# One 96-row transfer for each input chunk of a two-stage Fourier kernel, without zeroed gaps between its rows

## The chip, the cores and the metric

One core of a Trainium2 chip runs the kernel. The metric is the device time of one execution in microseconds; of several executions the median counts. Lower is better.

## The reference, cut to what is computed

A Fourier layer over 3008 positions (2 sequences, width 256) is followed by two feed-forward layers (6016 tokens, 256 to 2048 to 256):

```python
X = np.fft.rfft(x, axis=1)
Yr = Xr @ w_r - Xi @ w_i + b_r
Yi = Xr @ w_i + Xi @ w_r + b_i
# soft threshold of Yr and Yi at 0.01
y = np.fft.irfft(Y, n=x.shape[1], axis=1)
h = y @ w_in;   y = (h * np.cos(h)) @ w_out
h = y @ w_in2;  out = (h * np.clip(h + 3, 0, 6) / 6) @ w_out2
```

## The kernel before

The Fourier transform of length 3008 = 47 x 64 is done in two steps. The change touches the loads of the first one. For each sequence `b`, the input stands in memory as 96 rows (two groups `s` of 48, the even and the odd of each pair of columns) by 32 pairs by 256. It is read in 8 chunks of 4 pairs, numbered `a` = 0 to 15 over both sequences. A chunk has two pieces, `a_part(a, kc)`: four TensorE products (recorded as eight) of the chunk's rows with a trigonometric table `ta` of the same rows (line 544), one ScalarE eviction from PSUM (line 553) and, for the first sequence, one VectorE subtraction (line 555).

The table is block-diagonal: the row group `s` only meets the columns of its own `s`, and everything else in the table tile is zero. In the kernel before, the two row groups of a chunk are also put apart in the tile, rows 16 to 63 and 80 to 127 (kind 0) or rows 0 to 47 and 64 to 111 (kind 1), the kinds taking turns by pairs of chunks (`KINDS`, line 52). So each chunk takes two transfers of 48 rows (`load_x`, line 517), and the gap rows of both x and table are zeroed by VectorE, ScalarE and GpSimd before use (lines 568 to 596). The table of a pair of chunks also comes in two transfers, one per group (`load_ta`, line 526).

The first eight chunks (sequence 0) all have their own place: `x_big`, `x_ring[2]` and `ta_big`. They are loaded ahead and consumed one behind the other, pieces 0 to 15, before any other product. The next eight use rings of three (`XB`), are loaded by `load_next` and consumed one per step in `k2_step` (line 730), between the products `w_mm` (line 652), `b_mm` (674, 679) and `v_mm` (718).

The order of TensorE, SP and ScalarE is the program's own (`manual_schedule`, line 488); VectorE and GpSimd are left to the planner in this part. All loads but the first table pair, which ScalarE issues, are issued by SP in this order: x 0, x 1, table 2, x 2, x 3, table 4, x 4, x 5, table 6, x 6 (lines 597 to 603), two weights, x 7, two weights, then table and x of chunks 8 and 9, the constants, chunk 10, and the raw feed-forward weights. Before the first chunk, TensorE runs `WARM` products of the zeroed tile `warm` (line 607); no other work depends on them. After the Fourier part, the feed-forward layers run from about 160 us to the end as a sequence of products on TensorE (line 865).

Of the kernel before, what the change touches and what calls it, by code (L numbers as in the profile page):

```python
# [9 lines left out]
F32 = mybir.dt.float32  # L10
# [4 lines left out]
AF = mybir.ActivationFunctionType  # L15
# [6 lines left out]
NB, D, DFF = 2, 256, 2048  # L22
# [3 lines left out]
NPAIR = N2 // 2  # L26
TP = 2 * N1
ROWS = 2 * DOF
LAM = 0.01
TWO_PI = 2.0 * math.pi  # L30
YPAIRS = 4
A_CHUNKS = [4] * 8
NFC = DFF // 128
TILE = 128
WARM = 9
YT = YPAIRS * TP
NG = NB * NPAIR // YPAIRS

# [10 lines left out]
LASTC = 20  # L49
RATE_W = ((2, 1, 2), (1, 0, 1), (1, 1, 1), (0, 0, 0))  # L50
XB = 3
KINDS = (((16, 64), (80, 128), 128, ((0, 16), (64, 80)), (((0, 16), (64, 128)), ((0, 64), (64, 80)))), ((0, 48), (64, 112), 112, ((32, 64),), (((32, 64), (64, 128)), ((0, 64),))))
STAGED = [0] * 9 + [1, 2, 4, 5, 7, 8, 10] + [12] * 10
Y_EARLY = range(15, 18)
BIAS_DVE = range(13, 22)
# [25 lines left out]
def _tables():  # L81
    n1 = np.arange(N1)
    k2 = np.arange(NK2)
    ta = np.zeros((2, 48, NPAIR, NK2, 2))
    tg = np.zeros((2, NK2, 2, NPAIR, 2, N1))
    for i in range(NPAIR):
        for s in range(2):
            n = 64 * n1 + 2 * i + s
            c, sn = _trig(np.outer(n, k2), NSEQ)
            ta[s, :N1, i, :, 0] = c  # L90
            ta[s, :N1, i, :, 1] = -sn
            w = np.where(k2 == 0, 1.0, 2.0)[:, None] / NSEQ
            tg[s, :, 0, i, s, :] = w * c.T
            tg[s, :, 1, i, s, :] = -w * sn.T
    j = np.arange(N2)
    c, s = _trig(np.outer(j, j), N2)
    sg = np.where(j < N2 // 2, 1.0, -1.0)[None, :]
    f1 = np.zeros((2, N2, 2, N2))
    f1[0, :, 0], f1[1, :, 0] = c, s
    f1[0, :, 1], f1[1, :, 1] = -s, c  # L100
    f2 = np.zeros((2, N2, 2, N2))
    f2[0, :, 0], f2[1, :, 0] = sg * s, -sg * c
    f2[0, :, 1], f2[1, :, 1] = sg * c, sg * s
    g = np.zeros((2, N2, 2, 2, NPAIR))
    cc = c.reshape(N2, NPAIR, 2).transpose(0, 2, 1)
    ss = s.reshape(N2, NPAIR, 2).transpose(0, 2, 1)
    for z in range(2):
        g[0, :, z, 0], g[1, :, z, 0] = cc[:, z], -ss[:, z]
        g[0, :, z, 1], g[1, :, z, 1] = ss[:, z], cc[:, z]
    parts = []  # L110
    for m in (-f1, -f2, -g):
        parts += _split(m.reshape(128, 128))

    place = np.zeros((128, 128), dtype=np.float32)
    for row in (0, 32):
        place[row, :N2], place[row + 1, N2:] = -1.0, -sg[0]
    fg = np.concatenate(parts + [place], axis=1)
    return (
        ta.reshape(ROWS, NPAIR * 48).astype(np.float32),
        tg.reshape(ROWS, NPAIR * TP).astype(np.float32),  # L120
        np.ascontiguousarray(fg, dtype=np.float32),
    )
# [3 lines left out]
def fourier_moe_moe_kernel(ctx, tc, x, w_r, w_i, b_r, b_i, ta, tg, fg, win1, wout1, win2, wout2, out):  # L126
    nc = tc.nc
    pe, act, dve, sp = nc.tensor, nc.scalar, nc.vector, nc.sync

    def f32(ap):  # L130
        return ap.bitcast(F32)

    persist = ctx.enter_context(tc.tile_pool(name="persist", bufs=1))
# [352 lines left out]
    with ExitStack() as actx:  # L486
        apool = actx.enter_context(tc.tile_pool(name="apool", bufs=1))
        with tc.manual_schedule(engines={mybir.EngineType.PE, mybir.EngineType.SP, mybir.EngineType.Activation}):
# [2 lines left out]
            zl = apool.tile([128, NP, 2, 4, N2], F32R, name="zl")  # L491

            z1 = None
            x_big = persist.tile([128, 7, 4, D], F32, tag="zt", name="x_big")
            ta_big = persist.tile([128, 4, 2, 8, 48], F32, tag="wi0", name="ta_big")
            x_ring = [apool.tile([128, 4, D], F32, tag=f"x{r}", name=f"x_ring{r}") for r in range(XB)]
            ta_ring = [apool.tile([128, 2, 4, 48], F32, tag=f"ta{r}", name=f"ta_ring{r}") for r in range(XB)]
            a_list = []
            for b in range(NB):
                p0 = 0  # L500
                for n in A_CHUNKS:
                    a_list.append((b, p0, n))
                    p0 += n
            NA = len(A_CHUNKS)

            def place(a):

                if a >= NA:
                    r = (a - NA) % XB
                    return KINDS[r % 2], x_ring[r], ta_ring[r]  # L510
                xt = x_ring[XB - 1] if a == 0 else x_big[:, a - 1]
                return KINDS[a // 2 % 2], xt, ta_big[:, a // 2, :, 4 * (a % 2) : 4 * (a % 2) + 4]

            def load_x(a):
                b, p0, n = a_list[a]
                for s, (r0, r1) in enumerate(place(a)[0][:2]):
                    sp.dma_start(place(a)[1][r0:r1], x[b, 48 * s : 48 * s + 48, p0 : p0 + n, :])

            def load_ta(a, n, queue):
                p0 = a_list[a][1]  # L520
                kind, _, tt = place(a)
                if n > 4:
                    tt = ta_big[:, a // 2]
                for s, (r0, r1) in enumerate(kind[:2]):
                    src = ta[48 * s : 48 * s + 48, p0 * 48 : (p0 + n) * 48]
                    queue.dma_start(tt[r0:r1, s].rearrange("p i f -> p (i f)"), src)

            def load_next(a):
                if a < len(a_list):
                    load_ta(a, 4, sp)  # L530
                    load_x(a)

# [3 lines left out]
            def pool_zero(at):  # L536
                nc.gpsimd.memset(at, 0.0)

            def a_part(a, kc):
                b, p0, n = a_list[a]  # L540
                zp = h_bank(f"zp{a}_{kc}")
                (_, _, rows, _, _), xt, tt = place(a)
                for i in range(n):
                    pe.matmul(  # L544
                        zp[:, i * ROWS : (i + 1) * ROWS].rearrange("p (s f) -> p s f", s=2),
                        lhsT=xt[0:rows, i, kc * 128 : (kc + 1) * 128],
                        rhs=tt[0:rows, :, i],
                        start=True,
                        stop=True,
                    )  # L550
                src = zp[:, : n * ROWS].rearrange("p (n q f) -> p q f n", q=NP, f=4)
                dst = [z[:, :, kc, :, 2 * p0 : 2 * (p0 + n)] for z in ((zh, zl), (z1,))[b]]
                act.activation(dst[0], src, AF.Copy)
                if b == 0:
                    dve.tensor_tensor(dst[1], src, f32(dst[0]), op=ALU.subtract)

            def stage(q):

                act.activation(zh[:, q], z1[:, q], AF.Copy)
                pool_sub(zl[:, q], z1[:, q], f32(zh[:, q]))  # L560

            load_ta(0, 8, act)
            warm = persist.tile([128, 2, D], BF16, tag="r", bufs=5, name="warm")
            dve.memset(warm, 0.0)
            first = persist.tile([128, TILE], F32, tag="r", bufs=5, name="first")
            act.activation(first[:, 0:2], warm[:, 0, 0:2], AF.Sin)

            def x_zero(zero, kind, tiles):
                for r0, r1 in KINDS[kind][3]:
                    for t in tiles:  # L570
                        zero(t[r0:r1].rearrange("p n i e -> p (n i e)") if len(t.shape) == 4 else t[r0:r1].rearrange("p i e -> p (i e)"))

            def ta_zero(zero, kind, tile):
                for s in range(2):
                    for r0, r1 in KINDS[kind][4][s]:
                        zero(tile[r0:r1, s].rearrange("p i f -> p (i f)"))

            for t in (x_ring[2], x_big[:, 0]):
                for k, (r0, r1) in enumerate(KINDS[0][3]):
                    at = t[r0:r1].rearrange("p i e -> p (i e)")  # L580
                    if k == 0:
                        dve.memset(at, 0.0)
                    else:
                        act.activation(at, warm[r0:r1, 0, 0:1].to_broadcast([r1 - r0, 4 * D]), AF.Copy)
                if t is x_ring[2]:
                    ta_zero(dve_zero, 0, ta_big[:, 0])
            x_zero(pool_zero, 1, [x_big[:, 1:3]])
            ta_zero(pool_zero, 1, ta_big[:, 1])
            x_zero(pool_zero, 1, [x_big[:, 5:7]])
            ta_zero(pool_zero, 1, ta_big[:, 3])  # L590
            x_zero(pool_zero, 0, [x_big[:, 3:5]])
            ta_zero(pool_zero, 0, ta_big[:, 2])
            for r in range(XB):
                if r < XB - 1:
                    x_zero(pool_zero, r % 2, [x_ring[r]])
                ta_zero(pool_zero, r % 2, ta_ring[r])
            load_x(0)
            load_x(1)
            for a in range(2, NA):
# [5 lines left out]
            wp = psum.tile([128, 2, D], F32, tag="acc0", bufs=2, name="wp")  # L605
            for i in range(WARM):
                pe.matmul(wp, lhsT=warm[:, 0, 0:128], rhs=warm, start=True, stop=True)
# [212 lines left out]
    with tc.manual_schedule(engines=engines):  # L820
# [164 lines left out]
        for k in range(2 * G):  # L985
            n = HALF[k // STEPS % NJ]
            a, b, c, d = (bank(z, f"h{r}_{k}") for z, r in zip((0, 1, 2, 3) if k % 2 == 0 else (0, 3, 2, 1), "abcd"))
# [125 lines left out]
```

## Time and profile before

| | us |
|---|---|
| runs (three) | 1173.6, 1174.24, 1180.14 |
| median | 1174.24 |
| the profiled execution | 1174.77 |
| its span, first to last instruction | 1173.0 |

The profile shows one execution, with times from the start of the span. An engine's busy time counts neither issues of transfers nor waits. A stretch in which TensorE has gaps can be shortened; one without cannot, unless its own work shrinks. Transfers are shown by their issue on a queue (SPq, ACTq), by the median time from issue to landing, and by the rate at which all queues move bytes in a stretch. Names stand as out<-in.

### The profile page before, as it was taken

To read this page: it belongs to the slowest core of one execution; us is meant where nothing else is said; L and a number is where in the kernel's file an instruction comes from. 1 tells how busy PE (TensorE), PEld (TensorE's weight loads), DVE (VectorE), ACT (ScalarE), POOL (GpSimd) and SP (SyncE) were. 2 spreads that over 40 slices of the span, in tenths; PEclk is the share of its full clock that TensorE was granted. 3 is DMA by queue.
4 is the path that set the end of the run, shared out by engine and by line. 5 is a ranking of instruction groups with operands and counts; after the bars stand their busy time and mean duration, and the time that the engine had idled before them with its cause. 6 is when DMAs were issued, how large, how long until landed. Compare 5 with 4: busy or idle time off the path is not lost.

```text
span 1173.0 us, 15927 instructions
## 1 busy us (share of the span) xinstructions
PE 1154.8 (98%) x5363; PEld 965.8 (82%) x5363; DVE 766.5 (65%) x1096; ACT 814.7 (69%) x1548; POOL 814.3 (69%) x661
## 2 busy tenths in 40 slices
PE   8999989999999999999999999999999999999998
PEld 6887867778888888888888987888888888888897
DVE  5888877776679888988897677643343444433442
ACT  4677677777788888888788875565566556556554
POOL 5556636896787797888887786557757667577544
PEclk9999999999999999999999999999999999999999
DMA  9746639635413013104115420020020010100100
GB/s 202 194 115 178 190 95 292 211 100 171 136 55 110 34 59 130 37 18 149 37 39 187 172 93 1 1 72 1 1 72 1 19 54 1 68 1 1 37 1 32
DMA packets 48122, 98.71 MB, mean 84 GB/s; under 512 B 6436, under 2 KB 22952, under 8 KB 47400
## 3 DMA queue, kind: packets, MB, share of 16 engines
q1 hardware_dynamic: 47912, 97.54, 26.6%
q8 instruction: 42, 0.69, 0.3%
q14 instruction: 40, 0.33, 0.1%
q10 hardware_dynamic: 128, 0.15, 0.1%
HBM read 59.53 MB, written 38.14 MB: 83 GB/s over the span
## 4 chain that ended last, share of the span: by engine, by line
PE 85%; issue 4%; DMA 3%; POOL 3%; DVE 3%; ACT 2%; POOLq 0%; SPq 0%; ACTq 0%; DVEq 0%
PE acc L865 39%; PE hb L865 15%; PE ha L865 10%; PE hc L865 5%; PE hd L865 5%; PE pp L652 4%; POOL gl L175 3%; PE bp L679 2%; PE yp L391 2%; DMA x_big<-in_x_dram 1%; PE zp L544 1%; PE vp L718 1%; DVE r L841 0%; DMA ta_big<-in_ta_dram 0%; ACT tok L446 0%
## 5 line engine op out<-in xcount | busy, mean ns | idle before, releaser
L175 POOL TENSOR_TENSOR gl<-r,gh 128x512 fp32r<-128x512 f32 (+1 forms) x384 | 501.9, 1323 | 280.2 <-ACT gh L856 263.8
L865 PE MATMUL acc<-gh,wo 128*128 128x512 f32 (+1 forms) x1536 | 530.3, 386 | 0.0
L865 PEld LDWEIGHTS acc<-gh,wo 128*128 128x128 f32 x1536 | 288.6, 188 | 54.1
L865 PE MATMUL acc<-gl,wo 128*128 128x512 f32 (+1 forms) x768 | 296.1, 386 | 0.6 <-POOL gl L175 0.6
L865 PE MATMUL hb<-tok,wi 128*128 128x512 f32 (+1 forms) x864 | 241.7, 388 | 0.6 <-DVE hc L877 0.6
L856 ACT ACTIVATE gh<-r 128x512 fp32r<-128x512 f32 (+1 forms) x384 | 227.5, 615 | 0.4 <-PE acc L865 0.4
L865 PEld LDWEIGHTS hb<-tok,wi 128*128 128x128 f32 x864 | 161.3, 188 | 31.4 <-DVE hc L877 2.0
L877 DVE TENSOR_TENSOR hd<-p,hb 128x512 f32<-128x512 f32 (+1 forms) x96 | 65.8, 685 | 164.2 <-PE hb L865 159.3
L865 PEld LDWEIGHTS acc<-gl,wo 128*128 128x128 f32 x768 | 144.3, 188 | 27.6 <-POOL gl L175 1.0
L865 PE MATMUL ha<-tok,wi 128*128 128x512 f32 (+1 forms) x576 | 161.1, 388 | 2.2 <-ACT yo L410 2.2
L849 ACT ACTIVATE r<-r 128x512 f32<-128x512 f32 (+1 forms) x192 | 118.9, 619 | 57.3 <-DVE r L841 57.3
L865 PEld LDWEIGHTS ha<-tok,wi 128*128 128x128 f32 x576 | 108.0, 188 | 24.5 <-ACT yo L410 4.5
L449 POOL TENSOR_TENSOR tok<-st,tok 128x512 fp32r<-128x512 f32 (+1 forms) x77 | 97.7, 1282 | 2.9 <-ACT tok L446 2.9
L1006 ACT ACTIVATE p<-hc 128x512 f32<-128x512 f32 (+1 forms) x96 | 56.5, 588 | 58.4 <-PE hc L865 58.3
L843 ACT ACTIVATE r<-hd 128x512 f32<-128x512 f32 (+1 forms) x48 | 28.4, 591 | 78.1 <-PE hd L865 78.1
L997 ACT ACTIVATE hb<-ha 128x512 f32<-128x512 f32 (+1 forms) x96 | 55.2, 575 | 38.0 <-PE ha L865 37.8
L865 PE MATMUL hc<-tok,wi 128*128 128x512 f32 (+1 forms) x288 | 80.4, 387 | 1.2 <-DVE r L850 1.1
L865 PE MATMUL hd<-tok,wi 128*128 128x512 f32 (+1 forms) x288 | 79.7, 385 | 0.0
L877 DVE TENSOR_TENSOR hc<-p,hb 128x512 f32<-128x512 f32 (+1 forms) x96 | 65.4, 681 | 16.7 <-PE hb L865 15.9
L865 PEld LDWEIGHTS hc<-tok,wi 128*128 128x128 f32 x288 | 53.8, 188 | 12.5 <-DVE r L850 2.6
L865 PEld LDWEIGHTS hd<-tok,wi 128*128 128x128 f32 x288 | 54.1, 188 | 10.2
L850 DVE TENSOR_TENSOR r<-r,hb 128x512 f32<-128x512 f32 (+1 forms) x48 | 32.4, 675 | 40.9 <-ACT r L849 40.4
(144 smaller groups left out, 1712.8 us busy)
## 6 DMA issues: line engine op xcount, KB each, us to landing
st<-x_dram SPq DMA_DIRECT2D x18, 512.0 KB, 4.8
wi<-wi_dram SPq DMA_DIRECT2D x5, 1792.0 KB, 7.7
rawi<-in_win_dram SPq DMA_DIRECT2D x16, 512.0 KB, 4.0
rawo<-in_wout_dram SPq DMA_DIRECT2D x16, 512.0 KB, 3.8
u_dram<-v SPq DMA_DIRECT2D x48, 128.0 KB, 2.4
u_sb<-u_dram SPq DMA_DIRECT2D x16, 384.0 KB, 3.9
wo<-wo_dram SPq DMA_DIRECT2D x10, 512.0 KB, 8.0
x_dram<-o SPq DMA_DIRECT2D x20, 256.0 KB, 2.3
```

The source lines that it names most:

```text
L175: nc.gpsimd.tensor_tensor(out, x, y, op=ALU.subtract)
L391: pe.matmul(yp[:, i * TP : (i + 1) * TP], lhsT=u_sb[g][:, i, ec * 128 : (ec + 1) * 128], rhs=tg_sb[g][:, i * TP : (i + 1) * TP], start=Tru ...
L449: subtract(at(lo, t), src, f32(at(hi, t)), op=ALU.subtract)
L652: pe.matmul(pp.rearrange("p a e -> p (a e)"), lhsT=za[:, p, kc, 2 * (k2 % 2) : 2 * (k2 % 2) + 2, :].rearrange("p r n -> p (r n)"), rhs=wb[ ...
L843: act.activation(r, h, AF.Relu, bias=3.0, scale=1.0)
L849: act.activation(r, r, AF.Sin, bias=math.pi / 2, scale=1.0)
L850: dve.tensor_tensor(r, r, self.h[:, : self.n], op=ALU.mult)
L856: act.activation(gh[:, :n], self.r[:, :n], AF.Copy)
L865: pe.matmul(h[:, :n], lhsT=w, rhs=x, start=start and j == 0, stop=stop and j == 2, skip_group_check=True)
L877: dve.tensor_tensor(h[:, :n], r[:, :n], x[:, :n], op=ALU.add)
L997: act.activation(b[:, :n], a[:, :n], AF.Copy)
L1006: act.activation(p5[:, :n], c[:, :n], AF.Copy)
```

## The change

x and table rows of the two groups now stand directly behind each other, rows 0 to 47 and 48 to 95, in all chunks. A chunk of x is one transfer of 96 rows, and the x tiles have 96 rows and no gap rows. The table tiles keep zeros in the blocks off the diagonal: three memsets a tile, of which the first (rows 32 to 63 of group 0) overlaps rows that the load writes afterwards. The memsets of x are gone. `warm` is zeroed by GpSimd instead of VectorE, there are ten warm products instead of nine, and the table is laid out in memory pair by pair of chunks.

```diff
-WARM = 9
+WARM = 10
-        ta.reshape(ROWS, NPAIR * 48).astype(np.float32),
+        ta.reshape(ROWS, 4, NPAIR * 12).transpose(1, 0, 2).astype(np.float32),
...
-            x_big = persist.tile([128, 7, 4, D], F32, tag="zt", name="x_big")
+            x_big = persist.tile([ROWS, 7, 4, D], F32, tag="zt", name="x_big")
...
             def load_x(a):
-                b, p0, n = a_list[a]
-                for s, (r0, r1) in enumerate(place(a)[0][:2]):
-                    sp.dma_start(place(a)[1][r0:r1], x[b, 48 * s : 48 * s + 48, p0 : p0 + n, :])
+                sp.dma_start(place(a)[0], x[a // NA, :, 4 * (a % NA) : 4 * (a % NA) + 4])
 
             def load_ta(a, n, queue):
...
+                tt = place(a)[1] if n == 4 else ta_big[:, a // 2]
+                for s in range(2):
+                    src = ta[a % NA // 2, 48 * s : 48 * s + 48].rearrange("p (i f) -> p i f", f=48)
+                    queue.dma_start(tt[48 * s : 48 * s + 48, s], src if n == 8 else src[:, 4 * (a % 2) : 4 * (a % 2) + 4])
...
-                        lhsT=xt[0:rows, i, kc * 128 : (kc + 1) * 128],
-                        rhs=tt[0:rows, :, i],
+                        lhsT=xt[:, i, kc * 128 : (kc + 1) * 128],
+                        rhs=tt[:, :, i],
...
+            def ta_zero(zero, tile):
+                for r0, r1, s in ((32, 64, 0), (64, 96, 0), (0, 48, 1)):
+                    zero(tile[r0:r1, s].rearrange("p i f -> p (i f)"))
+
+            ta_zero(dve_zero, ta_big[:, 0])
             load_ta(0, 8, act)
             warm = persist.tile([128, 2, D], BF16, tag="r", bufs=5, name="warm")
-            dve.memset(warm, 0.0)
+            pool_zero(warm)
...
-            for t in (x_ring[2], x_big[:, 0]):
...
-            x_zero(pool_zero, 1, [x_big[:, 1:3]])
-            ta_zero(pool_zero, 1, ta_big[:, 1])
...
+            for k in (1, 2, 3):
+                ta_zero(pool_zero, ta_big[:, k])
             for r in range(XB):
-                if r < XB - 1:
-                    x_zero(pool_zero, r % 2, [x_ring[r]])
-                ta_zero(pool_zero, r % 2, ta_ring[r])
+                ta_zero(pool_zero, ta_ring[r])
```

## Rows read from the trace of the kernel before

**Rows 1.** The page's busy times: busy us (share of the span) xinstructions

```profile
PE 1154.8 (98%) x5363; PEld 965.8 (82%) x5363; DVE 766.5 (65%) x1096; ACT 814.7 (69%) x1548; POOL 814.3 (69%) x661
```

**Rows 2.** Windows: length, busy us by engine (xcount), PEclk, DMA share, GB/s

```profile
6.20:23.44 17.24, 15.21 (x128) 14.64 (x128) 8.59 (x16) 8.12 (x17) 11.45 (x22) 1.00 1.07 223
24.00:116.00 92.00, 91.03 (x462) 76.63 (x461) 76.46 (x110) 65.24 (x126) 50.83 (x40) 1.00 0.59 164
```

**Rows 3.** Chain of waits, 0 to 60 us: start us, us, what

```profile
4.95 5.09 DMA x_big<-in_x_dram
...
10.06 6.23 DMA x_big<-in_x_dram
...
16.30 5.26 DMA x_big<-in_x_dram
...
21.69 2.00 PE zp L544 x16
```

**Rows 4.** SP's own waits, 0 to 40 us: total us, times, longest us

```profile
SPq L526 <- DMA x_big<-in_x_dram: 3.6, 7, 0.7
```

**Rows 5.** Timeline, TensorE: start us, us, what xcount [idle before <-releaser]

```profile
1.20 4.02 PE L607 MATMUL wp<-warm 128*128 128x512 bf16 x9 [1.20 <-DVE warm L564]
6.21 2.00 PE L544 MATMUL zp<-ta_big,x_ring 128*128 128x96 f32 x16 [0.99 <-DMA ta_big<-in_ta_dram]
...
10.42 3.78 PE L544 MATMUL zp<-ta_big,x_big 112*128 112x96 f32 x32 [0.43 <-DVE zl L555]
...
21.69 2.00 PE L544 MATMUL zp<-ta_big,x_big 112*128 112x96 f32 x16 [0.80 <-DMA x_big<-in_x_dram]
23.47 0.48 PE L652 MATMUL pp<-wh,zh 128*128 128x512 f32 x1
```

**Rows 6.** Timeline of ScalarE, first unbroken run of evictions

```profile
8.24 0.49 ACT L553 ACTIVATE zh<-zp 128x384 fp32r<-128x384 f32 x1 [0.40 <-PE zp L544]
...
10.03 0.49 ACT L553 ACTIVATE zh<-zp 128x384 fp32r<-128x384 f32 x1 [0.40 <-PE zp L544]
```

**Rows 7.** DMA packets in 8 to 10 us, then in 1.8 to 23.4 us

```profile
DMA packets 132, 0.41 MB, mean 203 GB/s; under 512 B 33, under 2 KB 33, under 8 KB 132
...
DMA packets 2394, 4.76 MB, mean 220 GB/s; under 512 B 510, under 2 KB 1531, under 8 KB 2393
```

**Rows 8.** DMA in 32 to 33 us

```profile
DMA packets 101, 0.36 MB, mean 365 GB/s; under 512 B 12, under 2 KB 12, under 8 KB 101
```

**Rows 9.** A 96-row load; issues with KB and median us to landing; DMA 113.9:114.5

```profile
112.02 0.33 SPq L380 DMA_DIRECT2D u_sb<-u_dram  x1
...
u_sb<-u_dram SPq DMA_DIRECT2D x16, 384.0 KB, 3.9
...
x_big<-in_x_dram SPq DMA_DIRECT2D x14, 192.0 KB, 5.3
...
DMA packets 69, 0.21 MB, mean 356 GB/s; under 512 B 8, under 2 KB 22, under 8 KB 69
```

**Rows 10.** The start: timelines by engine, and one group with mean ns

```profile
0.74 0.90 ACTq L526 DMA_DIRECT2D ta_big<-in_ta_dram  x2
...
0.87 0.27 DVE L564 MEMSET warm<- 128x256 uint32 x1 [0.87 <-PEq L1099]
...
L534 DVE MEMSET ta_big<- 16x384 f32 x2 | 0.8, 378 | 0.1
...
0.74 1.80 POOL L537 MEMSET x_big<- 32x2048 f32 x1 [0.29 <-POOLq L1099]
2.48 1.36 POOL L537 MEMSET ta_big<- 32x384 f32 x3
```

**Rows 11.** DMA issues in 40 to 44 us: KB each, median us to landing

```profile
ta_ring<-in_ta_dram SPq DMA_DIRECT2D x1, 36.0 KB, 3.4
```

**Rows 12.** Busy times by stretch, later stages

```profile
176.60:180.00 3.40, 3.40 (x10) 2.64 (x9) 2.18 (x3) 2.94 (x7) 3.24 (x4) 0.50 0.96 330
...
140.00:260.00 120.00, 113.34 (x533) 91.16 (x532) 92.88 (x129) 89.25 (x171) 82.88 (x65) 0.99 0.58 185
```

More of the change, by code (lines that the diff above doesn't have):

```diff
@@ L31 @@
 YPAIRS = 4
-A_CHUNKS = [4] * 8
 NFC = DFF // 128
 TILE = 128
-WARM = 9
+WARM = 10
 YT = YPAIRS * TP
@@ L51 @@
 XB = 3
-KINDS = (((16, 64), (80, 128), 128, ((0, 16), (64, 80)), (((0, 16), (64, 128)), ((0, 64), (64, 80)))), ((0, 48), (64, 112), 112, ((32, 64),), (((32, 64), (64, 128)), ((0, 64),))))
 STAGED = [0] * 9 + [1, 2, 4, 5, 7, 8, 10] + [12] * 10
@@ L493, in fourier_moe_moe_kernel @@
             z1 = None
-            x_big = persist.tile([128, 7, 4, D], F32, tag="zt", name="x_big")
[L495 to L504, printed above, removed]
+            x_big = persist.tile([ROWS, 7, 4, D], F32, tag="zt", name="x_big")
+            ta_big = persist.tile([ROWS, 4, 2, 8, 48], F32, tag="wi0", name="ta_big")
+            x_ring = [apool.tile([ROWS, 4, D], F32, tag=f"x{r}", name=f"x_ring{r}") for r in range(XB)]
+            ta_ring = [apool.tile([ROWS, 2, 4, 48], F32, tag=f"ta{r}", name=f"ta_ring{r}") for r in range(XB)]
+            NA = NPAIR // 4
             def place(a):
@@ L509, in place @@
                     r = (a - NA) % XB
-                    return KINDS[r % 2], x_ring[r], ta_ring[r]
+                    return x_ring[r], ta_ring[r]
                 xt = x_ring[XB - 1] if a == 0 else x_big[:, a - 1]
-                return KINDS[a // 2 % 2], xt, ta_big[:, a // 2, :, 4 * (a % 2) : 4 * (a % 2) + 4]
+                return xt, ta_big[:, a // 2, :, 4 * (a % 2) : 4 * (a % 2) + 4]
             def load_x(a):
-                b, p0, n = a_list[a]
-                for s, (r0, r1) in enumerate(place(a)[0][:2]):
-                    sp.dma_start(place(a)[1][r0:r1], x[b, 48 * s : 48 * s + 48, p0 : p0 + n, :])
+                sp.dma_start(place(a)[0], x[a // NA, :, 4 * (a % NA) : 4 * (a % NA) + 4])
             def load_ta(a, n, queue):
[L520 to L526, printed above, removed]
+                tt = place(a)[1] if n == 4 else ta_big[:, a // 2]
+                for s in range(2):
+                    src = ta[a % NA // 2, 48 * s : 48 * s + 48].rearrange("p (i f) -> p i f", f=48)
+                    queue.dma_start(tt[48 * s : 48 * s + 48, s], src if n == 8 else src[:, 4 * (a % 2) : 4 * (a % 2) + 4])
             def load_next(a):
-                if a < len(a_list):
+                if a < 2 * NA:
                     load_ta(a, 4, sp)
@@ L539, in a_part @@
             def a_part(a, kc):
-                b, p0, n = a_list[a]
+                b, p0, n = a // NA, 4 * (a % NA), 4
                 zp = h_bank(f"zp{a}_{kc}")
-                (_, _, rows, _, _), xt, tt = place(a)
+                xt, tt = place(a)
                 for i in range(n):
@@ L560, in stage @@
                 pool_sub(zl[:, q], z1[:, q], f32(zh[:, q]))
+            def ta_zero(zero, tile):
+                for r0, r1, s in ((32, 64, 0), (64, 96, 0), (0, 48, 1)):
+                    zero(tile[r0:r1, s].rearrange("p i f -> p (i f)"))
+            ta_zero(dve_zero, ta_big[:, 0])
             load_ta(0, 8, act)
             warm = persist.tile([128, 2, D], BF16, tag="r", bufs=5, name="warm")
-            dve.memset(warm, 0.0)
+            pool_zero(warm)
             first = persist.tile([128, TILE], F32, tag="r", bufs=5, name="first")
             act.activation(first[:, 0:2], warm[:, 0, 0:2], AF.Sin)
[L568 to L576, printed above, removed]
-            for t in (x_ring[2], x_big[:, 0]):
[L579 to L586, printed above, removed]
-            x_zero(pool_zero, 1, [x_big[:, 1:3]])
-            ta_zero(pool_zero, 1, ta_big[:, 1])
[L589 to L592, printed above, removed]
+            for k in (1, 2, 3):
+                ta_zero(pool_zero, ta_big[:, k])
             for r in range(XB):
-                if r < XB - 1:
-                    x_zero(pool_zero, r % 2, [x_ring[r]])
-                ta_zero(pool_zero, r % 2, ta_ring[r])
+                ta_zero(pool_zero, ta_ring[r])
             load_x(0)
```

## Prediction

> **What bounds the kernel now.** I read the page's busy times first: TensorE is busy 1154.8 us of a span of 1173.0 [rows 1]. So a change outside TensorE can only give back TensorE's idle time. The busy times by stretch say where that is: from 24 us to 116 us it is busy 91.03 of 92.00, but from 6.20 to 23.44, the stretch that the diff edits, it is busy 15.21 of 17.24 while the DMA share is 1.07 [rows 2]. The chain of waits says what stands in the way there: three x transfers one behind the other, then TensorE from 21.69 [rows 3]. The reader is to see that each x transfer in that chain is issued within 0.02 us of the landing of the one before: a landing releases SP's next issue, so the stage is a closed loop at the pace of the DMA engines. SP's own waits say the same: seven waits of table issues for x landings, 3.6 us, lead the list [rows 4]. TensorE's order of time shows the stops: the first product at 6.21, then four stops, of which the first, before 10.42, and the last, before 21.69, stand there [rows 5]. Where nothing stops it, ScalarE's evictions start at 8.24 and, two pieces later, at 10.03: 0.895 us for each of the 16 pieces `a_part` [rows 6].
>
> **The price of an x chunk.** While only x pieces of 192 KB (48 rows) are in flight, the queues move 203 GB/s [rows 7]: 0.97 us for a half, 1.94 us for a chunk. TensorE needs two pieces for a chunk, 1.79 us, so the DMA is slower than TensorE, before the tables are counted. The same engines do better elsewhere: 365 GB/s at 32 us [rows 8]. The row closest to the new transfer is `u_sb`: 96 rows in one transfer, 384 KB, the same shape and row length. It lands 3.9 us after its issue, when a half of 192 KB takes 5.3 us in the loaded stage, and in the middle of the transfer issued at 112.02 the rate is 356 GB/s [rows 9]. (That rate may hold a little of the transfers around it: 22 of its 69 packets are small.) So a chunk costs between 1.08 us (at 365) and 1.94 us (no better than the halves). I take 1.10, the `u_sb` row, since shape and length are the same; but `u_sb` was nearly alone and x comes eight deep, so the upper bound stays in the range.
>
> [...]
>
> **Part by part.**
> *Loads.* x goes from two issues to one per chunk, about 0.45 us each by ScalarE's two [rows 10]; bytes do not change. Before the last chunk can be used, 8 chunks (3.15 MB), four table pairs (0.59 MB) and the first weights (0.26 MB) must pass: 4.0 MB. Fixed time around them, from the lone `u_sb`: 3.9 - 1.10 = 2.8 us [rows 9]. Before, at 220 GB/s over the stage [rows 7]: 0.75 + 2.8 + 18.2 = 21.75, and TensorE did restart at 21.69 [rows 5], so the model holds. After, at 356: 0.75 + 2.8 + 11.2 = 14.8. If TensorE starts at 6.0, it wants the chunk at 6.0 + 14 x 0.895 = 18.5. The loads then lie beside TensorE; that cover is gone below 4.0 MB / 14.95 us = 267 GB/s. What is late next is nothing before 18.5: TensorE's own pace becomes the bound.
>
> *First table.* Its zero rows 32 to 63 now overlap loaded rows 0 to 47, so ScalarE's first table issue waits for one VectorE memset (0.38 us, engine free at 0.87) [rows 10]: issue at 1.3 instead of 0.74, the second at 1.75 instead of about 1.2. Behind this wait in ScalarE's queue stand the activation table load and one tiny Sin; no eviction is due before 7. TensorE started 5.0 us after the old second issue; a lone table transfer takes 3.4 us [rows 11], so about 1.6 us was queueing at 220 GB/s; at 356 that is 1.0. Start: 1.75 + 3.4 + 1.0 = 6.15, with bounds 5.15 (alone) and 6.75 (as loaded as before). The ten warm products set a floor: GpSimd's memset of `warm` starts at 0.74 and costs between VectorE's 0.27 and the 0.45 of a 384-column one on GpSimd, and ten products at 4.02/9 = 0.447 us end near 5.6 [rows 5, 10]. I take 6.0. The tenth product, 0.45 us, fills time in which TensorE idled 0.99.
>
> *Later tables on SP.* Each first half waits for one GpSimd memset. GpSimd's big x memsets, the first from 0.74 for 1.80 us, are gone, so three memsets of 0.45 us a pair follow `warm` and the pairs 1 to 3 are zeroed at about 2.4, 3.8 and 5.1 [rows 10]. SP needs the first half-table of pair 1 at about 1.65, after two x issues, and the memset that it waits for (the first of three) ends near 1.6: at most 0.4 us for SP if the memsets run late, and behind that wait stand chunks 2 and 3, which TensorE wants at 9.6 and 11.4 and whose data lands 3 us earlier. The price is nothing; without that cover it would be the 0.4.
>
> *Memsets.* GpSimd sheds its x memsets, VectorE and ScalarE two each, all off TensorE's chain of [rows 3]: nothing, and nothing is uncovered. *Products* with 96 instead of 112 or 128 rows: 16 of 128 rows took 2.00 us at 6.21 and 16 of 112 rows 2.00 at 21.69 [rows 5], so the row count does not show: nothing, and by the same rows no loss either. *Table layout* by pairs: 1536-byte runs as before; taken as nothing, bounded by the table's whole 0.59 MB, 1.7 us, which the 3.7 us of slack above (18.5 - 14.8) covers.
>
> **The sum.** End of the stage: 6.0 + 16 x 0.895 + 0.1 = 20.4, against 21.69 + 2.00 = 23.69 [rows 5]; ScalarE must now squeeze two weight copies between evictions, +0.1. So -3.2 us. From 24 to 116 TensorE idles 1.0 us in all [rows 2], so the shift goes through; raw weights and constants are issued earlier too. Profiled execution: 1174.77 - 3.2 = 1171.6. It lies 0.5 over the median 1174.24, so **1171.0**.
>
> **The rivals.**
> *No relief (0.16).* Whole transfers also run at about 205 to 220 GB/s once several are queued, because the limit sits in the source rows or the queues. For it: x pieces never beat that in the stage. Against: `u_sb`. The last chunk is then again at about 21.7: time 1174.2, give or take 0.6.
> *Slower (0.05).* Transfers of 96 rows, queued one behind the other, crowd each other more than halves do, and a chunk costs more than two halves. It decides from 1.94 us per chunk; every 0.1 above costs 8 x 0.1 = 0.8 us at the same stops. At 2.4 us: 1174.2 + 3.7 = 1177.9. Against: `u_sb` [rows 9]. [...]
> *Table late (0.05).* The memset holds both halves of the first table and the queue is as full as before: the three memsets end near 2.2, 5.0 later is 7.2, the stage ends at 21.7, time 1172.2. The stage has no other place to lose it.
> *Later stages rearranged (0.08).* [...] Times from 1167.5 to 1176.
>
> **How the numbers follow.** The forecast has 0.66: 1170.5 to 1171.9 by the two starts, 5.6 and 6.75. With the late table, no relief and half of the last rival the range 1167.5 to 1174.8 holds a little over 8 in 10; the wrong-side rival lies outside. One per cent, about what a measurement of this kernel can tell from no change, is 11.7 us, more than every case gives: faster 0.02, same 0.96, slower 0.02.
>
> **What would show it.** Right: x landings under 5 us and over 267 GB/s between 3 and 15 us; zp without gaps from about 6.0, ending near 20.4; the first pp product near 20.2 instead of 23.47; all later stages 3 us earlier. Wrong: gaps before the fifth, ninth or thirteenth piece at 205 to 220 GB/s (no relief), a first product after 7 (table), or a shift of 3 us at 23 that is gone at 300 (later stages).

## The result

The changed kernel takes 1186.42 us (median of five runs, 1186.02 to 1188.27) against 1174.24 before; the ratio is 1.010, with a 95% interval of 1.0072 to 1.0128. The forecast was 3.2 us less, and the range up to 1174.8. The profiled execution took 1186.5 us, 11.7 more than that of before.

TensorE's timeline of the changed kernel, in the order of [rows 5] (start us, us, what xcount, idle before and who ended it):

```profile
1.32 4.45 PE L574 MATMUL wp<-warm 128*128 128x512 bf16 x10 [1.32 <-POOL warm L524]
7.60 2.13 PE L531 MATMUL zp<-ta_big,x_ring 96*128 96x96 f32 x16 [1.83 <-DMA ta_big<-in_ta_dram]
9.52 24.10 PE L531 MATMUL zp<-ta_big,x_big 96*128 96x96 f32 x112
33.33 0.77 PE L619 MATMUL pp<-wh,zh 128*128 128x512 f32 x1
```

The ten warm products end at 5.77, TensorE then stands idle for 1.83 us, and the last of the 16 pieces ends at 33.62, where it ended at 23.69 before. There are no more stops between chunks: at this pace of TensorE the loads keep up. What is longer is the work itself: 112 products in 24.10 us, which is 1.72 us a piece where [rows 6] gave 0.895. ScalarE's evictions, which follow the pieces, show the same, 1.71 us apart:

```profile
9.77 0.49 ACT L540 ACTIVATE zh<-zp 128x384 fp32r<-128x384 f32 x1 [0.53 <-PE zp L531]
11.47 0.49 ACT L540 ACTIVATE zh<-zp 128x384 fp32r<-128x384 f32 x1 [1.22 <-PE zp L531]
13.18 0.49 ACT L540 ACTIVATE zh<-zp 128x384 fp32r<-128x384 f32 x1 [1.22 <-PE zp L531]
```

The windows (length, busy us by engine, PEclk, DMA share, GB/s) say why:

```profile
6.00:9.30 3.30, 1.70 (x15) 1.73 (x16) 0.03 (x1) 0.49 (x1) 1.86 (x8) 1.00 1.04 260
9.40:36.60 27.20, 27.20 (x123) 26.62 (x123) 10.09 (x18) 8.73 (x18) 0.00 (x0) 0.50 0.71 193
36.70:128.70 92.00, 90.17 (x465) 76.56 (x464) 76.79 (x110) 64.59 (x125) 52.39 (x42) 1.00 0.50 144
```

TensorE's granted clock is 1.00, the upper level of this trace, in the row from 6.00 to 9.30, then 0.50, the lower level, for 27 us, with TensorE busy all the time, and 1.00 again from 36.65, 3.3 us after the wide weight products began. Before, nothing of the kind stands in this stage: the clock was 1.00 through [rows 2].

The views read 1.00 before 6 us too, but the warm products took as long as products of their shape do at 0.50. The weight products, 128x512 as well, took 628 ns each (median) under 0.50, from 33.85 to 36.05, and 389 to 397 ns under 1.00, from 37.4 to 60 us. The warm products (busy us, mean ns): the ten of the changed kernel, then five that ran between 5.0 and 5.9 us in a kernel with 13 of them (further down):

```profile
L574 PE MATMUL wp<-warm 128*128 128x512 bf16 x10 | 4.4, 631 | 1.3 <-POOL warm L524 1.3
```

```profile
L575 PE MATMUL wp<-warm 128*128 128x512 bf16 x5 | 1.2, 379 | 0.0
```

So the 1.00 that the views give at the start of this trace does not agree with the length of the products, 631 ns.

In the whole program the stage accounts for nearly all of it: its end moved by 9.9 us, the end of the first six weight products by 10.7 (36.24 against 25.59), the execution by 11.7.

The first table, for which that first product waits, took 5.7 us from issue to landing instead of 4.8 and was issued about 0.5 us later. DMA issues by ScalarE in the first 9 us, KB each, median us to landing, first of the changed kernel, then of the kernel before:

```profile
ta_big<-in_ta_dram ACTq DMA_DIRECT2D x2, 72.0 KB, 5.7
```

```profile
ta_big<-in_ta_dram ACTq DMA_DIRECT2D x2, 72.0 KB, 4.8
```

And the pace of the loads did rise, though not to the 356 GB/s of [rows 9]. DMA packets from 2 to 18 us, of the changed kernel, of the kernel before, and of the changed kernel's stretch with x transfers almost alone (10.2 to 12.2 us):

```profile
DMA packets 1892, 4.14 MB, mean 259 GB/s; under 512 B 303, under 2 KB 1139, under 8 KB 1892
```

```profile
DMA packets 1524, 3.42 MB, mean 214 GB/s; under 512 B 357, under 2 KB 863, under 8 KB 1524
```

```profile
DMA packets 138, 0.48 MB, mean 242 GB/s; under 512 B 18, under 2 KB 21, under 8 KB 138
```

### The profile page after: what moved, and what is told of

Its sections match the earlier page's. It is cut to its first block, busy times and chain, and to the rows that moved or that the text cites. A ratio compares the mean times of both kernels' runs of the same rounds, so it can differ in the third digit from the quotient of the medians.

```text
span 1184.7 us, 15891 instructions
## 1 busy us (share of the span) xinstructions
PE 1166.3 (98%) x5364; PEld 978.4 (83%) x5364; DVE 764.3 (65%) x1092; ACT 811.7 (69%) x1546; POOL 804.0 (68%) x652
## 4 chain that ended last, share of the span: by engine, by line
PE 85%; issue 4%; POOL 4%; ACT 2%; DVE 2%; DMA 2%; POOLq 0%; SPq 0%; ACTq 0%; DVEq 0%
PE acc L832 38%; PE hb L832 14%; PE ha L832 10%; PE hc L832 5%; PE hd L832 5%; PE pp L619 4%; PE zp L531 3%; POOL gl L173 3%; PE bp L646 2%; PE yp L389 2%; PE vp L685 1%; DMA ta_big<-in_ta_dram 0%; DVE r L808 0%; DMA wo<-wo_dram 0%; DMA tg_sb<-in_tg_dram 0%
## 5 line engine op out<-in xcount | busy, mean ns | idle before, releaser
L964 ACT ACTIVATE hb<-ha 128x512 f32<-128x512 f32 (+1 forms) x96 | 55.2, 575 | 37.5 <-PE ha L832 37.4
L832 PEld LDWEIGHTS hc<-tok,wi 128*128 128x128 f32 x288 | 53.7, 188 | 12.5 <-DVE r L817 2.5
L176 POOL TENSOR_TENSOR w<-cvai,cvbi 128x512 f32<-128x512 f32 x16 | 21.4, 1335 | 59.9 <-DVE cvbi L215 59.9
```

The source lines that it names most:

```text
L832: pe.matmul(h[:, :n], lhsT=w, rhs=x, start=start and j == 0, stop=stop and j == 2, skip_group_check=True)
L964: act.activation(b[:, :n], a[:, :n], AF.Copy)
```

## The experiments

Two theories stood against each other. *Gap*: TensorE's idle time between the warm products and the first chunk, 1.83 us instead of 0.99, made the clock fall. *Narrow work*: products of 96 rows, where there were 112 and 128, made it fall. A second question was what made the first table late: the memset that it now waits for, or the whole transfers ahead of it. Each kernel was measured beside the kernel before on the same chip.

### More warm products

```diff
-WARM = 10
+WARM = 17
```

> The changed kernel with 17 warm products instead of 10, nothing else. They should end near 7.3 us, so that TensorE no longer stands idle for 1.83 us before the first chunk. Gap theory (the clock fell because TensorE stood still between the warm products and the first chunk): granted clock 1.00 through the first stage, first product at 7.6, the 16 pieces at 0.895 us each, the first weight product near 22 instead of 33.6, and a time near 1174.2 - 1.7 = 1172.5. Rival, narrow-work theory (products of 96 rows are too little work for the clock, whatever stands before them): the clock falls again within a few us of the first chunk, time near 1186.

Measured: 1172.79 us against 1175.83, ratio 0.9977 (0.9964 to 0.9990), and no run of ten above 1175.2. TensorE's timeline, and the stage's window:

```profile
1.32 6.52 PE L574 MATMUL wp<-warm 128*128 128x512 bf16 x17 [1.32 <-POOL warm L524]
7.68 1.92 PE L531 MATMUL zp<-ta_big,x_ring 96*128 96x96 f32 x16
9.44 12.67 PE L531 MATMUL zp<-ta_big,x_big 96*128 96x96 f32 x112
21.89 0.48 PE L619 MATMUL pp<-wh,zh 128*128 128x512 f32 x1
```

```profile
7.70:21.90 14.20, 14.20 (x130) 14.20 (x128) 8.27 (x15) 7.93 (x17) 0.48 (x2) 1.00 1.05 270
```

With the gap filled and nothing else altered, 96-row products ran for 14 us at 1.00, at 0.89 us a piece (14.21 us from the first to the weight product), and the loads, at 270 GB/s, made no stop between chunks at this pace either. So narrow work alone did not make the clock fall. The stage ends at 22.1, which is what the forecast's own formula gives for a start at 7.68.

### The gap in the kernel before

The first try at a gap moved ScalarE's issue behind its Sin in the program:

```diff
-            load_ta(0, 8, act)
...
             act.activation(first[:, 0:2], warm[:, 0, 0:2], AF.Sin)
+            load_ta(0, 8, act)
```

> The kernel before, with the first table pair issued by ScalarE after its Sin instead of before it, about 2.4 us later; rows and transfers of x as before. The first chunk should start near 8 instead of 6.2, the gap after the warm products grows from 1.0 to 2.5 or 3 us. Gap theory: the clock falls to 0.50 here too, with products of 112 and 128 rows; the first stage ends 8 us or more later, time 1184 to 1188. Narrow-work theory: the clock stays at 1.00, and since the stage waits for the x transfers anyway, time 1174 to 1176.

Measured: 1176.48 us against 1175.83, ratio 1.0004 (0.9989 to 1.0019). It told little: the issue moved only from 0.74 to 1.18, since ScalarE's queue did not wait for the Sin that stands ahead of it in the program and ran from 2.04 to 2.24. The first product started at 6.33, 1.11 us after the warm products, and the clock stayed at 1.00. The second try made the transfer wait for a memset that overlaps it, as in the change:

```diff
-            load_ta(0, 8, act)
...
-                    ta_zero(dve_zero, 0, ta_big[:, 0])
+                    dve_zero(ta_big[0:32, 0, 0].rearrange("p i f -> p (i f)"))
+                    load_ta(0, 8, act)
...
```

> The kernel before, with the first table's transfer behind a VectorE memset that overlaps its rows (rows 0 to 31 instead of 0 to 15 are zeroed first), so that it is issued near 2.6 instead of 0.74; halves of x, 112 and 128 rows as before. The first product should start near 8, the gap after the nine warm products grows from 1.0 to about 2.5 us. Gap theory: the clock falls here too, the stage of 16 pieces runs at 1.5 us each, time 1185 to 1190. Narrow-work theory in its weaker form (96-row products cannot hold the clock over a gap, 112 and 128 can): clock 1.00, 1174 to 1177.

Measured: 1177.64 us against 1175.79, ratio 1.0017 (1.0008 to 1.0026). Its timeline and windows:

```profile
1.20 4.02 PE L609 MATMUL wp<-warm 128*128 128x512 bf16 x9 [1.20 <-DVE warm L563]
8.03 2.75 PE L544 MATMUL zp<-ta_big,x_ring 128*128 128x96 f32 x16 [2.81 <-DMA ta_big<-in_ta_dram]
10.57 13.59 PE L544 MATMUL zp<-ta_big,x_big 128*128 128x96 f32 x112
```

```profile
5.70:9.00 3.30, 0.97 (x9) 1.00 (x9) 0.00 (x0) 0.00 (x0) 3.17 (x5) 1.00 1.09 216
9.10:12.40 3.30, 3.30 (x18) 3.30 (x17) 1.12 (x2) 0.98 (x2) 3.10 (x5) 0.50 1.08 216
12.60:24.00 11.40, 11.40 (x105) 11.40 (x104) 7.11 (x13) 6.81 (x14) 5.32 (x14) 1.00 1.04 217
```

After 2.81 us of idleness the clock fell at 9.1 here as well, so 96-row products were not needed for the fall. But it was back at 12.5, and the loss was about 2 us. All products that ran between 9.1 and 12.5 us were those of chunks 0 and 1, over 128 rows; the 112-row ones came later:

```profile
L544 PE MATMUL zp<-ta_big,x_big 128*128 128x96 f32 x10 | 2.2, 403 | 0.0
L544 PE MATMUL zp<-ta_big,x_ring 128*128 128x96 f32 x9 | 1.9, 393 | 0.0
```

Neither theory had this: with the gap the clock fell in both kernels, and something in the changed kernel kept it down.

### Rows of the products

All transfers, the memset wait and the ten warm products as in the change, but tiles of 128 rows with zeros in rows 96 to 127:

```diff
...
-            x_big = persist.tile([ROWS, 7, 4, D], F32, tag="zt", name="x_big")
+            x_big = persist.tile([128, 7, 4, D], F32, tag="zt", name="x_big")
...
-                sp.dma_start(place(a)[0], x[a // NA, :, 4 * (a % NA) : 4 * (a % NA) + 4])
+                sp.dma_start(place(a)[0][0:ROWS], x[a // NA, :, 4 * (a % NA) : 4 * (a % NA) + 4])
...
-                for r0, r1, s in ((32, 64, 0), (64, 96, 0), (0, 48, 1)):
+                for r0, r1, s in ((32, 64, 0), (64, 128, 0), (0, 48, 1), (96, 128, 1)):
...
```

> The changed kernel with its first-stage products over 128 rows: rows 96 to 127 of the x and table tiles are zeroed by VectorE and GpSimd, the transfers, the memset wait, the ten warm products and so the gap of about 1.8 us stay. Row theory (the gap makes the clock fall with any products, but 96-row products cannot bring it back, and 112- and 128-row products can, as in the kernel before with the gap, where it came back after 3.4 us): the clock falls near 7.5 to 9.5, is back at 1.00 within about 4 to 7 us, the stage ends near 24 to 26, time 1175 to 1179. If the row count has no part in it (the whole transfers or the different pace of the loads kept the clock down): it stays at 0.50 until the wide weight products, time 1185 to 1188.

Measured: 1176.69 us against 1175.14, ratio 1.0007 (0.9993 to 1.0021); ten runs between 1172.4 and 1180.1. The profiled one was the slowest of them:

```profile
1.32 4.45 PE L583 MATMUL wp<-warm 128*128 128x512 bf16 x10 [1.32 <-POOL warm L524]
8.32 3.70 PE L531 MATMUL zp<-ta_big,x_ring 128*128 128x96 f32 x16 [2.55 <-DMA ta_big<-in_ta_dram]
11.81 13.79 PE L531 MATMUL zp<-ta_big,x_big 128*128 128x96 f32 x112
```

```profile
14.20:25.40 11.20, 11.20 (x103) 11.20 (x102) 7.16 (x13) 6.51 (x15) 2.19 (x9) 1.00 1.04 252
```

The gap was 2.55 us, and the first 16 products took 3.70 us, where they took 2.00 at 1.00 [rows 5]; from their start to that of the next group it is 0.218 us each, and the changed kernel's took 0.215 at 0.50 (112 in 24.10). So by their length the clock was down from the first product on, though the view read 1.00 from 8.3 to 12 us. From 14.2 us their length agrees with 1.00: 103 products fill 11.2 us, 0.109 us each. With 96 columns and the same transfers, zeros in 32 more rows let the clock come up within 6 us of the first product, where the changed kernel's clock stayed down to the end of the 16 pieces; none of the ten runs lies above 1180.1, and all five of the changed kernel lie at 1186 or more. The only other edit is the memsets of the added rows. So the row count is what kept the clock down in this stage, and it did not matter that the added rows hold zeros. Where between 96 and 128 rows this turns was not measured.

### Wide products in the middle

The changed kernel with 14 more warm products between pieces 4 and 5:

```diff
+                    if (c, kc) == (1, 1):
+                        for i in range(14):
+                            pe.matmul(wp, lhsT=warm[:, 0, 0:128], rhs=warm, start=True, stop=True)
```

> The changed kernel with 14 more wide products of the zeroed tile between the fourth and the fifth piece of the first stage, where the clock is already down; nothing else. They cost 14 x 0.43 = 6 us at the low clock. If the narrow products of the stage are what keeps the clock down once it has fallen (it came back only when the wide weight products began), it comes back during or just behind the 14 products, near 20 us, the other 12 pieces run at 0.9 instead of 1.5 us, and the time is near 1186.5 + 6 - 7 = 1185 to 1186, with granted clock 1.00 from about 20 us instead of 36.6. If the clock stays down for a set time whatever runs, it is still 0.50 until 36 us and the time is near 1192.

Measured: 1178.98 us against 1175.79, ratio 1.0032 (1.0022 to 1.0042), that is 7 us under the changed kernel although it does 5 us more work. Windows:

```profile
6.40:9.70 3.30, 2.13 (x19) 2.16 (x20) 0.47 (x1) 0.59 (x2) 1.51 (x6) 1.00 1.03 274
9.80:16.50 6.70, 6.48 (x23) 4.21 (x24) 1.67 (x3) 1.27 (x3) 0.00 (x0) 0.50 1.04 286
16.60:28.00 11.40, 11.40 (x99) 10.95 (x98) 5.85 (x11) 5.77 (x13) 0.00 (x0) 1.00 0.92 264
```

The inserted products, over 128 rows and 512 columns, brought the clock back by 16.6 us, and the 96-row pieces behind them held it at 1.00 to their end. So the clock did not stay down for a set time: 27 us in the changed kernel, under 7 here. What TensorE ran brought it back.

### What made the table late

Without the memset wait: the first half of the first table is loaded with 16 rows of zeros behind it.

```diff
...
-                    src = ta[a % NA // 2, 48 * s : 48 * s + 48].rearrange("p (i f) -> p i f", f=48)
+                    r = 64 if a == 0 and s == 0 else 48
+                    src = ta[a % NA // 2, 64 * s : 64 * s + r].rearrange("p (i f) -> p i f", f=48)
...
-            ta_zero(dve_zero, ta_big[:, 0])
+            ta_zero(dve_zero, ta_big[:, 0], 1)
```

> The changed kernel, but the first table's transfer does not wait for a memset: its first half brings 16 rows of zeros along (64 rows instead of 48), so that ScalarE issues it at 0.74 as in the kernel before. If the memset wait (0.55 us) is what makes the table late, it lands near 6.3 to 6.6, the first chunk starts near 6.7, the gap is about 1 us as in the kernel before, the clock holds, and the time is near 1171.5. If the whole x transfers ahead in the queues make it late, it still lands near 7.2, the gap is near 1.5 us or more, and under the gap theory the clock may fall as before: near 1186. Narrow-work theory: 1185 to 1186 either way.

Measured: 1188.59 us against 1175.83, ratio 1.0107 (1.0085 to 1.0129). Its two transfers, in the columns used above:

```profile
ta_big<-in_ta_dram ACTq DMA_DIRECT2D x1, 96.0 KB, 5.6
ta_big<-in_ta_dram ACTq DMA_DIRECT2D x1, 72.0 KB, 6.5
```

They were issued from 0.75 on, but the second, for which the first product waits, landed no earlier. From the chain of waits (start us, us, what), first of the changed kernel, then of this one:

```profile
1.72 5.75 DMA ta_big<-in_ta_dram
```

```profile
1.33 6.51 DMA ta_big<-in_ta_dram
```

It landed at 7.85 instead of 7.47, and the first product came at 7.98. So the memset wait alone was not the cause. Next, x in halves again, everything else as in the change:

```diff
-                sp.dma_start(place(a)[0], x[a // NA, :, 4 * (a % NA) : 4 * (a % NA) + 4])
+                for s in range(2):
+                    sp.dma_start(place(a)[0][48 * s : 48 * s + 48], x[a // NA, 48 * s : 48 * s + 48, 4 * (a % NA) : 4 * (a % NA) + 4])
```

> The changed kernel with each x chunk in two transfers of 48 rows again (rows 0 to 47 and 48 to 95), nothing else: the row count of the products, the memset wait and the ten warm products stay. If the whole transfers make the first table late, it lands near 6.5 here, the gap is near 1 us, and under the gap theory the clock holds: 1172 to 1175. If the memset wait makes it late, the first chunk starts at 7 or later and the clock falls: 1185 to 1188. Narrow-work theory: 1186 either way.

Measured: 1186.99 us against 1175.83, ratio 1.0097 (1.0071 to 1.0124). The table landed in 4.4 us and the first product came at 6.95, 0.65 earlier; but in this execution the ten warm products took 3.79 us instead of 4.45 and were over at 5.11, the gap was 1.84 us again, and the clock fell. (In three of the eight runs of this kernel and the one above, the mean granted clock is 0.997 or 0.998 and not 0.985 to 0.986, although they took as long; they were not traced.) DMA packets from 2 to 18 us:

```profile
DMA packets 1798, 3.95 MB, mean 247 GB/s; under 512 B 401, under 2 KB 1044, under 8 KB 1798
```

This is 247 GB/s, with halves, where the kernel before had 214 with halves in other rows and the changed kernel 259. How the gain splits is not shown. One execution each is a weak basis: the kernel above, with whole transfers, moved 248 in the same window. And the rows are not all that differs from the kernel before: the memsets of x and the table's layout do too. The memsets seem to have a share, for the kernel with 128 rows has the changed kernel's transfers, zeroes 32 more rows of each tile, and moved 238:

```profile
DMA packets 1632, 3.80 MB, mean 238 GB/s; under 512 B 272, under 2 KB 912, under 8 KB 1632
```

Last, the order on SP:

```diff
             load_x(0)
+            load_ta(2, 8, sp)
             load_x(1)
             for a in range(2, NA):
-                if a % 2 == 0:
+                if a % 2 == 0 and a > 2:
                     load_ta(a, 8, sp)
```

> The changed kernel with two issues swapped on SP: the table of chunks 2 and 3 goes ahead of x chunk 1, nothing else. Queue theory (transfers are served about in the order of their issue over both queues, so the first table waits behind two whole chunks, 768 KB, where in the kernel before it waited behind one, 384 KB): the table lands 1.4 us earlier, near 6.0 instead of 7.47, the first product starts near 6.1, the gap after the warm products is near 0.4 us, the clock holds at 1.00, the stage ends near 20.5 to 21.5 and the time is 1171 to 1172.5. If the memset wait or a fixed time of the transfer makes the table late: first product at 7.3 or later, a gap above 1.5 us, the clock falls, 1185 to 1188.

Measured: 1174.19 us against 1175.79, ratio 0.9993 (0.9971 to 1.0015), ten runs from 1171.1 to 1175.3 and one of 1187.8. TensorE's timeline, and ScalarE's DMA issues in the columns used above:

```profile
1.32 3.78 PE L575 MATMUL wp<-warm 128*128 128x512 bf16 x10 [1.32 <-POOL warm L524]
6.03 2.00 PE L531 MATMUL zp<-ta_big,x_ring 96*128 96x96 f32 x16 [0.92 <-DMA ta_big<-in_ta_dram]
8.71 12.88 PE L531 MATMUL zp<-ta_big,x_big 96*128 96x96 f32 x112 [0.68 <-DMA x_big<-in_x_dram]
```

```profile
ta_big<-in_ta_dram ACTq DMA_DIRECT2D x2, 72.0 KB, 4.1
```

With one whole x chunk instead of two issued ahead of it, the table landed 4.1 us after the same issue and the first product came at 6.03, 1.6 us earlier. So the table was late because a second whole chunk had been issued ahead of it. The order of issue is not all of it: without the memset wait, the table's first half was issued at 0.75 together with chunk 0 and ahead of chunk 1, and still took 5.6 us. So in these runs ScalarE's own queue did not bring the table past SP's x.

This run also tests the gap with the warm-up unchanged: ten warm products, 0.92 us of idle time instead of 1.83, and the 112 products of 96 rows then took 12.88 us, with the clock at 1.00, instead of 24.10.

### Versions that go past both kernels

Both edits for the table at once:

> Both edits at once: the first table brings 16 rows of zeros along and waits for no memset, and the table of chunks 2 and 3 goes ahead of x chunk 1. Queue theory: first product near 5.8 (the ten warm products end near 5.8 or earlier), clock 1.00, time 1171 to 1172.5, at most 0.3 us under the kernel with the swap alone. Wait theory: this one holds the clock and the swap alone does not.

Measured: 1174.35 us against 1175.79, ratio 1.0017 (0.9983 to 1.0051). The profiled execution started at 5.74 and held the clock, but four of twelve runs took 1186 to 1187.5. Then the swap on SP with `WARM = 13`:

> The changed kernel with the table of chunks 2 and 3 ahead of x chunk 1 on SP, and 13 warm products instead of 10. The table lands near 5.9, the warm products end between 6.0 and 6.5, so nothing stands between them and the first chunk. Gap and row theory: the clock is 1.00 through the stage in all runs (the swap alone had one run of eleven above 1187), first product near 6.3, the first weight product near 20.9 to 21.4, time 1170.5 to 1172, under both kernels. If the slow runs of the kernels with the swap come from something else than the gap, some runs here lie near 1187 too.

Measured: 1172.81 us against 1175.14, ratio 0.9980 (0.9958 to 1.0003), one run of eleven at 1184.2. With `WARM = 17`:

> The changed kernel with the table of chunks 2 and 3 ahead of x chunk 1, and 17 warm products. With 13 one run of eleven was at 1184 with a mean granted clock of 0.988. If that run is the gap and the small stop before chunk 1 met by an early end of the warm products, 17 products, which end between 6.4 and 7.5 us, leave neither: no run above 1178, first product between 6.5 and 7.5, time 1171 to 1173. If slow runs come from elsewhere, about one in ten stays near 1185.

Measured: 1172.55 us against 1175.88, ratio 0.9970 (0.9959 to 0.9981), no run above 1176.4. And the swap, 13 warm products and products over 128 rows:

> The changed kernel with the table of chunks 2 and 3 ahead of x chunk 1, 13 warm products and products over 128 rows (rows 96 to 127 zeroed). Row theory: even where the clock falls or has not yet risen, the 128-row products bring it to 1.00 within a few us, so no run lies above 1180; undisturbed runs at 1171 to 1173 as with 96 rows. If row count has no part: as with 96 rows and 13 warm products, one run in ten near 1185.

Measured: 1172.46 us against 1175.88, ratio 0.9980 (0.9971 to 0.9990), eleven runs from 1170.9 to 1176.1. (In its profiled execution the loads moved 241 GB/s from 2 to 18 us, against 264 with 96 rows and 13 warm products, and TensorE stopped for them again, 0.60 and 0.61 us.) By their intervals these last two are faster than the kernel before by 0.1 to 0.4%, and none of their runs comes near the changed kernel's 1186; the same holds for the change with `WARM = 17` alone, and between the three the intervals do not decide. The six runs above 1184 us of the three kernels with the swap and ten or thirteen warm products were not traced. Three of them have a mean granted clock of 0.986 to 0.988, as the changed kernel has, and three have 0.998, so it is not shown that the clock fell in all of them.

## Why the prediction was wrong

**The step that failed** is the sum's silent premise that TensorE's pace in this stage, 0.895 us a piece, would hold. Its rows show the clock at 1.00 in the stage [rows 2]; the one low stretch among them, 0.50 for 3.4 us from 176.6, lies in a later one [rows 12]. It wrote of the row count "so the row count does not show", from products of 112 and 128 rows at 1.00. That was true of their duration: at 1.00, with 17 warm products, those of 96 rows took 0.89 us a piece. What the rows could not show was what 96-row products do once the clock is down. The runs put it at 11.5 us: 1.72 us a piece until the wide products come, so that the stage ended at 33.62 where it ended at 22.11 with 17 warm products and nearly the same start.

**The term that was mis-sized** and set it off is the start: 6.0 forecast, 7.60 measured, outside its bounds of 5.15 to 6.75. The upper bound was "as loaded as before" and left out that two whole chunks, not one, would be issued ahead of the table. The 3.4 us of its "lone table transfer" were also those of a 36 KB transfer [rows 11], when the halves of the first table have 72 KB. The wait for the memset, to which the prediction gave the delay, was as short as worked out (issue at 1.29, forecast 1.3) and, by the run without it, costs nothing. The rival "table late" had the start at 7.2 and the time at 1172.2, still 2 us under the kernel before; it had the right place, the wrong cause (the three memsets) and no clock in it. The tenth warm product "fills time in which TensorE idled 0.99", said the prediction; with the later start it left 1.83.

**The price of a chunk** was 1.10 us forecast; 242 GB/s with x almost alone makes it 1.62 us (393 KB). The lone `u_sb` transfer, 356 GB/s, was a poor guide to transfers that queue eight deep (in the changed kernel eight were issued by 3.5 us, the ninth at 5.18). The stage moved 259 GB/s where it had moved 214. That is under the 267 at which TensorE was to wait for loads, but TensorE began later: at its full pace and a start at 7.68, no stop between chunks was left.

**What held:** the loads stopped being the bound; TensorE's pace is the bound behind them; the memset that the first table waits for cost nothing, by the run without it; and, with the gap filled, the stage ended where the formula puts it and the time fell by 0.23%, 2.7 us, the size of the forecast's 3.2. The chance for slower by over 1%, 0.02, was too small: the point estimate lies at 1.010. No run shows a rearrangement of later stages that would give the times of that rival, 1167.5 to 1176, of which the lower is also that of the range: in the changed kernel TensorE idled 7.0 us from 140 to 260 us, where it had idled 6.7, with the clock at 1.00, and no run of any kernel here took under 1170.69.

## What to carry to other kernels

When a change moves the first real work of TensorE, work out the idle time that it leaves behind the warm-up (here 1.83 us), and price a fall of the clock over the whole stage that follows (11.5 us), not over the gap. Ask then whether that stage's products can bring the clock back: here products over 96 rows did not in 24 us, and the same products over 128 rows, with zeros added, did within 6. A merged transfer also puts more bytes ahead of what is issued behind it, here on another queue too (the table landed in 5.7 us behind two whole chunks, in 4.1 behind one), so let the small transfer that the first product needs go ahead of the second large one.

## What was not expected of the hardware

In the executions profiled, the granted clock fell to 0.50 after an idle time of 1.83 us between two runs of products, and did not after 0.92, 0.99 and 1.11 us. With 17 warm products the clock stayed at 1.00 for 14 us of products over 96 rows, but it did not rise from 0.50 in 24 us of their unbroken work, while under products over 128 rows, in the kernel before with a gap of 2.81 us, it was 0.50 from 9.1 to 12.4 and 1.00 from 12.6. ScalarE's queue issued a transfer at 1.18 us that stands behind an activation that ended at 2.24. And the loads of x in rows 0 to 47 and 48 to 95 moved 247 GB/s in halves, where the kernel before moved 214, with other rows, memsets and table layout, in one execution each.
